# Filler products of 128 columns instead of 512 in a fused attention and feed-forward kernel

## The chip, the cores and the metric

The kernel runs on one core of one Trainium2 chip. The metric is the time of one execution on the device, in microseconds (us), as the median of several runs. The engines are TensorE (PE in the profile; its weight loads are PEld), VectorE (DVE), ScalarE (ACT), GpSimd (POOL) and SyncE (SP). Each has a queue of its own and works it off in order; they wait for each other by semaphores. TensorE writes its products into PSUM, which has eight banks; another engine must read a bank before TensorE may write it again.

## The reference

Two layers, each applied twice: memory-augmented attention in four segments, and a gated feed-forward block, both with a layer norm ahead and a residual sum behind. x is 2048 rows of 512 columns, there are 32 heads of 16 columns, and the feed-forward block is 1792 wide; everything is bfloat16. Cut to what matters:

```python
def A(x, wq, wk, wv, wo, beta):                 # x: 1 x 2048 x 512; 4 segments of 512 rows
    q, k, v = heads(x @ wq), heads(x @ wk), heads(x @ wv)
    phi = lambda t: where(t > 0, t + 1.0, exp(t))
    g = sigmoid(beta)
    for s in range(4):                          # M, z start at zero
        p = softmax(qs @ ks.T * scale + causal_mask)
        a_mem = (phi(qs) @ M) / (phi(qs) @ z + 1e-06)
        o = g * a_mem + (1.0 - g) * (p @ vs)
        M = M + phi(ks).T @ vs
        z = z + sum(phi(ks))
    return o @ wo

def B(x, w_gate, w_up, w_down):
    return (gelu(x @ w_gate) * (x @ w_up)) @ w_down

x = x + A(layernorm(x)); x = x + B(layernorm(x))
x = x + A(layernorm(x)); x = x + B(layernorm(x))
```

## The kernel before

The rows of x are worked in 8 pieces `k` = 0 to 7: four segments of 512 rows, in each of the two passes. For every piece there is an attention part (`Att`) and a feed-forward part (`Ffn`), and the parts of several pieces run interleaved, so that TensorE always has something to multiply while ScalarE works on the exponentials of the attention.

What TensorE does for a piece, in the names of the program:

- the query, key and value products (`wq_sb`, `wk_sb`, `wv_sb` with the normed and transposed rows `xnT`), by `product` (lines 471 and 476);
- the scores, `score_round` (line 938): small products of 16 or 32 rows that run side by side in strips of the array. They write four banks at a time, ScalarE takes their exponential into `pt` (line 1396), GpSimd or VectorE masks it (lines 1343, 1348, 1353);
- the flush, `flush_item` (line 954): `pt` times the values `vaug` and `vz`, in four columns of the array. VectorE turns the result (`byq`, line 971) and divides it by the sums;
- the memory's update, `upd_item`, which multiplies `phik` and the values; `phik` is turned by a DMA from SP (line 437). VectorE makes `mblk` of it and copies it to `macc` (line 893);
- the output product with `wo_sb`, the gate, up and down products with `wg_sb`, `wu_sb` and `wd_sb`; ScalarE or VectorE evicts the gate (`evict`, lines 461 and 462);
- turns of normed rows by TensorE itself for some pieces (`turn_item`, lines 584 and 586): two products of 256 columns that nobody reads, four transposes, and so on. ScalarE or VectorE then copies the result to `xnT`.

The order on every engine is written out when the kernel is built. `order` runs a model of the five engines: `ck.pe` is the planned time of TensorE, each product adds its planned cost (`Clocks.MM`, 0.2158 us for 512 columns, 0.056 for 128), and the other engines' jobs get planned times from their own costs. The main loop (from line 1423) picks what TensorE does next: scores when two rounds are ready and ScalarE has little left, else the next product of the open item, else a new item with a free bank. Changing between whole products, rows and columns of the array is planned at 0.109 us.

Where nothing is ready by the plan, a bank is free and scores are still to come (`streams` is not empty), the loop lays in a product that nobody reads: `warm` (128 x 128, all ones) times `wide`, which is `warm` read four times over, 512 columns into the free bank (line 1462). If the array stands in columns, or is about to, `product` cuts it into four products of 32 columns of the array that run side by side, each with 512 columns of data. The plan adds 0.2158 us and marks the bank as free again just after. Where no bank is free or no scores are left, the plan moves on by 0.05 us without a product.

At the start, 15 products of the same kind are made ahead of the first data (`keep_warm`, line 349); these and the ones in the turns (line 584) are not touched.

Of the kernel before, what the change touches and what calls it, by code (L numbers as in the profile page):

```python
# [18 lines left out]
P = 128  # L19
# [266 lines left out]
def order(pol, nc, cst, seg, wrk, psp, A_x, A_wq, A_wk, A_wv, A_wo, A_beta, B_x, B_w_gate, B_w_up, B_w_down, out):  # L286
# [51 lines left out]
    warm = cst.tile([P, P], BF16, name="warm")  # L338
    wide = warm[:].unsqueeze(1).to_broadcast([P, 4, P])
# [125 lines left out]
    def product(out, lhsT, rhs, start=True, stop=True):  # L465

        if ck.mode == "columns" or ck.mode == "rows" and (any(it.kind == "flush" and it.near() for it in items)):
            ck.tiling("columns")
            for c in range(4):
                r = slice(32 * c, 32 * c + 32)  # L470
                nc.tensor.matmul(out[r], lhsT=lhsT[:, r], rhs=rhs, start=start, stop=stop, tile_position=(0, 32 * c))  # L471
            ck.count += 4
        else:
            ck.tiling("whole")
            ck.count += 1
            nc.tensor.matmul(out, lhsT=lhsT, rhs=rhs, start=start, stop=stop)  # L476
# [797 lines left out]
    def next_e():  # L1274
        if not e_slots.free or e_slots.queue or phase[0] is not None:
            return
        now = streams[0][0] + streams[0][1] / STEPS if streams else 1e9
        act = ck.act
        idle = act.free <= ck.pe and act.table == "exp" and not act.only and not any(j[0] <= ck.pe and not j[4] for j in act.jobs)
        got = [j for j in e_jobs if j[1] <= ck.pe and j[2]() and (idle or j[0] <= now)]  # L1280
        if got:
            job = min(got, key=lambda j: j[0])
            e_jobs.remove(job)
            job[3](job[1], pol.e_slack)
            ck.serve()
# [17 lines left out]
    def tight():  # L1303

        return any(slot_free[slot_of(k, t)] is None for k, t in streams[2:4])
# [7 lines left out]
    def rounds_now(idle=False):  # L1313

        if not streams or phase[0] is not None and phase[1] > pol.hold or not rounds_ready(2):
            return 0
        n, left = len(free_pairs()), len(streams)
        wait = backlog()
        if n >= 2 and (idle or left <= 4 or wait < (pol.early if streams[0][0] < 1 else pol.starve)):
            return 2  # L1320
        return 0

    def pick():

        got = [i for i in range(BANKS) if banks[i] <= ck.pe]
        if not got:
            return None
        mine = sum(banks[i] > ck.pe for i in range(BANKS) if i not in score_banks)
        if streams and mine >= pol.cap and backlog() < pol.near and rounds_ready(2):
            return None  # L1330
        apart = {i for i in range(BANKS) if i not in score_banks and banks[i] > ck.pe + pol.soon} if streams else ()
        return min(got, key=lambda i: (-len(pairs_of(set(range(BANKS)) - {i, *apart})), banks[i]))

    def open_item(got, bank):
        it = min(got, key=lambda it: it.due())
        items.remove(it)
        it.ps.bank = bank
        banks[bank] = 1e9
        return it
# [83 lines left out]
    while streams or items or opened or ck.busy():  # L1423
        assert ck.pe < 2000.0, (streams[:1], [(it.kind, it.due()) for it in items[:9]], e_jobs[:2], banks)
        pol.move(ck.pe)
        ck.dve.shun = pol.shun
        ck.serve()
        next_e()
        n = rounds_now()
        if n:  # L1430
            score(n)
            continue
        if opened:
            cost, fn = opened.ops.pop(0)
            fn()
            ck.on_pe(cost)
            if not opened.ops:
                it, opened = opened, None
                it.done()
            continue  # L1440
        bank = pick()
        if bank is not None:
            late = ck.pe - pol.flush_wait
            for ck.back in (pol.lag, 0.0):
                got = [it for it in items if it.after in ev and it.ready() and (
                    it.kind != "flush" or not streams or tight() or it.posted < late or ck.mode == "columns")]
                if got:
                    break
            ck.back = 0.0
            if got:  # L1450
                opened = open_item(got, bank)
                continue

        n = rounds_now(True)
        if n:
            score(n)
            continue
        if bank is not None:
            if streams:
                ps = Psum()  # L1460
                ps.bank = bank
                product(ps(), warm[:], wide)
                ck.on_pe(Clocks.MM[512])
                ps.read(ck.pe)
                ck.fills.append(ck.pe)
                continue
        ck.pe += 0.05
        ck.stalls.append(ck.pe)
# [3 lines left out]
@with_exitstack  # L1472
def kernel(
    ctx: ExitStack,
    tc: tile.TileContext,
    A_x: bass.AP,
    A_wq: bass.AP,
    A_wk: bass.AP,
    A_wv: bass.AP,
    A_wo: bass.AP,  # L1480
    A_beta: bass.AP,
    B_x: bass.AP,
    B_w_gate: bass.AP,
    B_w_up: bass.AP,
    B_w_down: bass.AP,
    out: bass.AP,
):
    cst = ctx.enter_context(tc.tile_pool(name="cst", bufs=1))
    seg = ctx.enter_context(tc.tile_pool(name="seg", bufs=1))
    wrk = ctx.enter_context(tc.tile_pool(name="wrk", bufs=2))  # L1490
    psp = ctx.enter_context(tc.tile_pool(name="psp", bufs=1, space=bass.MemoryType.PSUM))
    ctx.enter_context(tc.manual_schedule(engines=MANUAL))
    order(Policy(POLICY, CHANGES), tc.nc, cst, seg, wrk, psp, A_x, A_wq, A_wk, A_wv, A_wo, A_beta, B_x, B_w_gate, B_w_up, B_w_down, out)
# [31 lines left out]
```

## Time and profile before

| | |
|---|---|
| time, median of 3 runs | 546.05 us (546.04 to 547.07) |
| the profiled execution's own time | 545.75 us |
| its span, first to last instruction | 544.0 us |
| mean granted clock of TensorE in it | 0.999 |
| TensorE busy | 531.3 us (98% of the span) |
| VectorE busy | 443.7 us (82%) |
| ScalarE busy | 434.7 us (80%) |
| GpSimd busy | 305.5 us (56%) |

The profile is one execution. A matmul's row shows when it started and how long it took until its last result; the next one starts before that, so the distance from start to start is what a product costs in a dense stream. A row of the timeline merges instructions of one kind that follow each other: start, time from the first start to the last end, engine and line, output and inputs, shape, count, and in brackets the idle time ahead of it with what ended it. What is named there is the last semaphore event before the start; it need not be the one that was needed. In the chain of waits the profile goes back from the last instruction, at each step to what released it or to its predecessor on the same engine. Some records of matmuls are missing (9273 products stand beside 9334 weight loads). The windows give, for a stretch, its length, the busy time and count of an engine, the mean granted clock, and the DMA engines' share and rate.

### The profile page before, as it was taken

To read this page: it belongs to the slowest core of one execution; us is meant where nothing else is said; L and a number is where in the kernel's file an instruction comes from. 1 tells how busy PE (TensorE), PEld (TensorE's weight loads), DVE (VectorE), ACT (ScalarE), POOL (GpSimd) and SP (SyncE) were. 2 spreads that over 40 slices of the span, in tenths; PEclk is the share of its full clock that TensorE was granted. 3 is DMA by queue.
4 is the path that set the end of the run, shared out by engine and by line. 5 is a ranking of instruction groups with operands and counts; after the bars stand their busy time and mean duration, and the time that the engine had idled before them with its cause. 6 is when DMAs were issued, how large, how long until landed. Compare 5 with 4: busy or idle time off the path is not lost.

```text
span 544.0 us, 21276 instructions
## 1 busy us (share of the span) xinstructions
PE 531.3 (98%) x9273; PEld 276.3 (51%) x9334; DVE 443.7 (82%) x816; ACT 434.7 (80%) x540; POOL 305.5 (56%) x359
## 2 busy tenths in 40 slices
PE   8999999999999999999999999999999999999997
PEld 4454555454545444554545555545465456555444
DVE  6998999799988999779987998889586797786342
ACT  5999989988898989989899798996879977920330
POOL 4898786369746788339993468716753265300000
PEclk9999999999999999999999999999999999999999
DMA  8406511610331123310312250221320114100001
GB/s 249 117 13 192 118 20 13 176 33 22 45 56 21 26 40 58 44 40 7 41 32 49 33 72 3 41 32 23 78 52 3 22 21 82 24 3 22 19 0 40
DMA packets 64926, 26.95 MB, mean 50 GB/s; under 512 B 49216, under 2 KB 64832, under 8 KB 64832
## 3 DMA queue, kind: packets, MB, share of 16 engines
q1 hardware_dynamic: 64400, 25.31, 22.6%
q8 instruction: 73, 1.20, 0.9%
q10 hardware_dynamic: 432, 0.27, 0.2%
q14 instruction: 21, 0.17, 0.1%
HBM read 9.71 MB, written 2.10 MB: 22 GB/s over the span
## 4 chain that ended last, share of the span: by engine, by line
PE 88%; DVE 7%; DMA 2%; issue 2%; ACT 0%; ACTq 0%; SPq 0%; DVEq 0%
PE ps L476 46%; PE ps L471 26%; PE ps L938 8%; PE ps L954 7%; DVE st L514 1%; DVE x_sb L1027 1%; DMA beta_bc<-in_A_beta_dram 1%; DVE byq L971 1%; PE ps L586 1%; DVE phiq L745 1%; PE ps L584 1%; DMA phik<-e 0%; DMA amT<-am 0%; DVE xn L544 0%; DVE e L764 0%
## 5 line engine op out<-in xcount | busy, mean ns | idle before, releaser
L1396 ACT ACTIVATE pt<-ps 128x1024 bf16<-128x1024 f32 x288 | 278.9, 1025 | 44.6 <-PE ps L938 41.1
L1343 POOL TENSOR_SCALAR_AFFINE_SELECT pt<-pt 128x256 bf16<-128x256 bf16 (+1 forms) x192 | 107.0, 571 | 118.0 <-ACT pt L1396 112.0
L1092 DVE TENSOR_TENSOR gel_sb<-gel_sb,ps 128x512 bf16<-128x512 bf16 x112 | 75.3, 682 | 33.9 <-PE ps L476 25.0
L476 PE MATMUL ps<-xnT,wu_sb 128*128 128x512 bf16 x287 | 66.8, 379 | 1.4 <-issue 1.1
L476 PE MATMUL ps<-xnT,wg_sb 128*128 128x512 bf16 x261 | 62.6, 379 | 0.9 <-issue 0.5
L764 POOL TENSOR_SCALAR e<-e 128x512 bf16<-128x512 bf16 x37 | 57.9, 1565 | 1.8 <-ACT e L741 0.7
L971 DVE STREAM_TRANSPOSE byq<-ps 128x512 f32<-128x512 f32 x64 | 45.0, 706 | 16.5 <-PE ps L954 15.9
L476 PE MATMUL ps<-wd_sb,gel_sb 128*128 128x512 bf16 (+1 forms) x293 | 56.8, 340 | 1.3 <-issue 1.0
L1348 POOL TENSOR_SCALAR_AFFINE_SELECT pt<-pt 64x1024 bf16<-64x1024 bf16 x40 | 47.8, 1196 | 15.0 <-ACT pt L1396 13.7
L1027 DVE TENSOR_TENSOR x_sb<-x_sb,ps 128x512 bf16<-128x512 bf16 (+1 forms) x68 | 42.8, 640 | 16.3 <-PE ps L476 14.7
L471 PE MATMUL ps<-wd_sb,gel_sb 128*32 128x512 bf16 (+1 forms) x792 | 47.1, 378 | 0.3 <-issue 0.3
L476 PEld LDWEIGHTS <-wu_sb 128*128 128x128 bf16 x301 | 28.2, 98 | 33.8 <-issue 0.7
L471 PE MATMUL ps<-xnT,wg_sb 128*32 128x512 bf16 x700 | 42.4, 380 | 0.0
L514 DVE BATCH_NORM_STATS2 st<-x_sb 128x6 f32<-128x512 bf16 x60 | 40.4, 674 | 0.4 <-DMA x_sb<-in_A_x_dram 0.3
L476 PEld LDWEIGHTS <-wg_sb 128*128 128x128 bf16 x273 | 25.3, 98 | 28.8 <-issue 0.2
L476 PEld LDWEIGHTS <-gel_sb 128*128 128x128 bf16 x306 | 28.3, 98 | 22.7 <-issue 1.1
L954 PE MATMUL ps<-pt,vaug 128*32 128x256 bf16 (+2 forms) x1344 | 34.6, 238 | 0.0
L417 POOL TENSOR_SCALAR kx<-kf,masks 128x512 bf16<-128x512 bf16 x20 | 33.5, 1678 | 1.2
L471 PE MATMUL ps<-xnT,wu_sb 128*32 128x512 bf16 x588 | 34.1, 379 | 0.0
L1151 ACT ACTIVATE gel_sb<-gel_sb 128x2048 bf16<-128x2048 bf16 (+1 forms) x21 | 33.2, 1643 | 0.0
L544 DVE TENSOR_SCALAR xn<-x_sb,mv,rs 128x512 bf16<-128x512 bf16 x58 | 31.3, 592 | 2.2 <-POOL rs L532 1.9
L954 PEld LDWEIGHTS <-vaug 128*32 128x32 bf16 x1344 | 27.8, 97 | 10.4 <-issue 2.2
(147 smaller groups left out, 883.6 us busy)
## 6 DMA issues: line engine op xcount, KB each, us to landing
vz<-vaug SPq DMA_DIRECT2D x14, 136.0 KB, 2.9
wg_sb<-in_B_w_gate_dram SPq DMA_DIRECT2D x8, 224.0 KB, 4.6
wu_sb<-in_B_w_up_dram SPq DMA_DIRECT2D x8, 224.0 KB, 4.3
wd_sb<-in_B_w_down_dram SPq DMA_DIRECT2D x7, 256.0 KB, 4.2
x_sb<-in_A_x_dram SPq DMA_DIRECT2D x3, 512.0 KB, 7.3
out_dram<-x_sb SPq DMA_DIRECT2D x12, 128.0 KB, 1.8
xnT<-xn SPq DMA_TRANSPOSE x40, 2.5
wk_sb<-in_A_wk_dram SPq DMA_DIRECT2D x2, 256.0 KB, 6.0
```

What stands on the lines that cost most here:

```text
L471: nc.tensor.matmul(out[r], lhsT=lhsT[:, r], rhs=rhs, start=start, stop=stop, tile_position=(0, 32 * c))
L476: nc.tensor.matmul(out, lhsT=lhsT, rhs=rhs, start=start, stop=stop)
L514: nc.vector.bn_stats(out=self.st6[:, 0, :], in_=x_sb[:, self.tt0 + j, :])
L764: lambda eng: eng.tensor_scalar(out=e[0][:], in0=e[0][:], scalar1=1.0, scalar2=None, op0=ALU.min), summed)
L938: nc.tensor.matmul(ps_all[:, bank, o + c0:o + c0 + n], lhsT=lhsT, rhs=self.q[rows, b, q0:q0 + n], start=True, stop=True, tile_position=(32 ...
L954: nc.tensor.matmul(ps()[32 * j:32 * j + 32, q0:q0 + n], lhsT=va[:, ki * VW + g:ki * VW + g + 32], rhs=pt_all[:, places[i], j, c0:c0 + n], ...
L971: nc.vector.transpose(out=self.byq[:, par, :, :].rearrange("p a c -> p (a c)"), in_=ps()[:])
L1027: ck.dve.post(ck.made(), slack, (0.15 + 0.00104 * (c1 - c0), lambda: nc.vector.tensor_tensor(out=xt, in0=xt, in1=ps()[:, 0:c1 - c0], op=AL ...
L1092: ck.dve.post(ck.made(), NORMAL, (0.683, lambda: nc.vector.tensor_tensor(out=g, in0=g, in1=ps()[:], op=ALU.mult), lambda t: (ps.read(t), e ...
L1343: nc.gpsimd.affine_select(out=view, in_=view, pattern=[[0, 4], [0, n], [1, C]], compare_op=ALU.is_ge, fill=0.0, base=C, channel_multiplier=-1)
L1348: nc.gpsimd.affine_select(out=view, in_=view, pattern=[[0, 4 * TPS], [1, C]], compare_op=ALU.is_ge, fill=0.0, base=0, channel_multiplier=-1)
L1396: nc.scalar.activation(out=pt_all[:, s0:s0 + 2, 2 * p:2 * p + 2, :].rearrange("p r h c -> p h r c"), in_=ps_all[:, pair[0]:pair[1] + 1, :] ...
```

## The change

The product that is laid in where the plan has nothing else takes 128 columns of `warm` instead of 512, and writes the first 128 columns of the bank. The planned cost stays that of 512 columns, so the plan, and with it the number, place and order of all instructions on all engines, stay as they were: 19 whole products and 48 in columns (12 groups of four) have a shorter operand, and that is the only difference between the two programs.

```diff
             if streams:
                 ps = Psum()
                 ps.bank = bank
-                product(ps(), warm[:], wide)
+                product(ps()[:, 0:P], warm[:], wide[:, 0, :])
                 ck.on_pe(Clocks.MM[512])
                 ps.read(ck.pe)
                 ck.fills.append(ck.pe)
```

## The prediction

> **What bounds the kernel now.** I read the page first, then the group of the products that read `warm`, then the chain of waits from 70 to 82 us, the timeline around every place where these products stand, and last the windows with the granted clock.
>
> ```profile
> span 544.0 us, 21276 instructions
> ...
> PE 531.3 (98%) x9273; PEld 276.3 (51%) x9334; DVE 443.7 (82%) x816; ACT 434.7 (80%) x540; POOL 305.5 (56%) x359
> ...
> PEclk9999999999999999999999999999999999999999
> ...
> PE 88%; DVE 7%; DMA 2%; issue 2%; ACT 0%; ACTq 0%; SPq 0%; DVEq 0%
> ```
>
> TensorE is busy for 98% of the span and carries 88% of the chain that ended last, at full clock. So time taken out of TensorE's stream is time gained, but only where the next product doesn't wait for somebody else. That is the whole question here: the products that are shortened (I call each a fill) stand exactly where the program's author expected nothing else to be ready.
>
> ```profile
> L471 PE MATMUL ps<-warm x48: 377/379/380, 73.8 to 135.7; 128*32 128x512 bf16 x48
> ...
> L476 PE MATMUL ps<-warm x19: 376/379/390, 21.8 to 140.1; 128*128 128x512 bf16 x19
> ```
>
> These are all of them: 19 whole fills and 48/4 = 12 that are cut into four columns of the array, 31 in all, between 21.8 and 140 us. After 140 us there is none, so the last 400 us can only inherit what is gained before.
>
> ```profile
> 69.46 2.45 DMA phik<-e
> 71.91 0.05 issue
> ...
> 73.56 1.73 PE ps L471 x50
> 75.29 0.33 PE ps L938 x12
> 75.62 1.40 PE ps L476 x6
> ...
> 79.93 0.22 PE ps L586 x4
> 80.15 0.65 PE ps L476 x3
> ```
>
> In this chain the fills lie on the path: 75.62 is six of them, 80.15 is three (0.65/3 = 0.216 us each, first start to next start). Four products of 128 columns take 0.22 us (79.93), 0.055 each. The chain says what ended last, not what would be late next.
>
> **The change part by part.** Number, places and order of all instructions stay; the planner still charges the long cost, so nothing else moves on any queue, SP's and POOL's included. One fill costs 0.216 - 0.056 = 0.160 us less, so the gross saving is 31 x 0.160 = 4.96 us. In column mode the four run side by side, so a group counts once: (1.47 - 0.38)/5 = 0.22 us per group in the row at 73.82 below. What is left is found place by place, by following each wait behind a fill to the instruction that it needs.
>
> ```profile
> 33.19 0.38 PE L586 MATMUL ps<-ident,xn 128*128 128x128 bf16 x4 [0.26 <-DVE byq L971]
> ...
> 72.98 1.94 ACT L1396 ACTIVATE pt<-ps 128x1024 bf16<-128x1024 f32 x2 [0.46 <-PE ps L938]
> ...
> 73.82 1.47 PE L471 MATMUL ps<-warm 128*32 128x512 bf16 x24
> 75.22 0.40 PE L938 MATMUL ps<-q,kf 16*128 16x64 bf16 x12
> 75.55 1.47 PE L476 MATMUL ps<-warm 128*128 128x512 bf16 x6
> ...
> 76.95 0.67 DVE L893 COPY macc<-ps 128x512 f32<-128x512 f32 x1
> ...
> 77.95 0.29 PE L938 MATMUL ps<-q,kf 16*128 16x64 bf16 x8
> ```
>
> *Two fills at 21.8.* At most 0.32 us; TensorE then sits idle at 33.19 for DVE (0.26). Taken as 0.
>
> *Three fills just before the memory update.* Behind them the update's weights wait for the transposed `phik`, which lands at 71.91 (the chain's first rows). 0.48 us becomes idle time there: 0. If that transfer came earlier, the ceiling is 0.48.
>
> *Six groups at 73.82, six whole fills at 75.55.* Gross 12 x 0.160 = 1.92. After the first six the scores need banks that the exponentials leave at 72.98 + 1.94 = 74.92; with 0.05 for the wait they begin at 74.97 instead of 75.22: 0.25 left. After the next six the flush may begin early, but the scores behind it need the bank that DVE's L893 copies out until 76.95 + 0.67 = 77.62. They begin at 77.66 instead of 77.95: 0.29 us left of 1.92. DVE runs this copy in its own order behind work that no fill feeds, so it doesn't move.
>
> ```profile
> 78.47 1.94 ACT L1396 ACTIVATE pt<-ps 128x1024 bf16<-128x1024 f32 x2 [0.28 <-PE ps L938]
> 80.30 0.60 ACT L462 ACTIVATE xnT<-ps 128x512 bf16<-128x512 bf16 x1
> ...
> 80.73 0.40 PE L938 MATMUL ps<-q,kx 32*128 32x256 bf16 x12
> 81.06 0.39 PE L476 MATMUL ps<-warm 128*128 128x512 bf16 x1
> 81.29 0.38 PE L476 MATMUL ps<-xnT,wg_sb 128*128 128x512 bf16 x1
> ...
> 86.79 1.02 ACT L1396 ACTIVATE pt<-ps 128x1024 bf16<-128x1024 f32 x1 [0.71 <-PE ps L938]
> ...
> 91.42 0.63 ACT L462 ACTIVATE gel_sb<-ps 128x512 bf16<-128x512 f32 x1
> ...
> 91.91 0.61 PE L476 MATMUL ps<-xnT,wg_sb 128*128 128x512 bf16 x2
> ```
>
> *Three fills at 79.98, one at 81.06.* Gross 0.64 on top of 0.29. ACT's exponentials at 78.47 wait for the scores, so ACT is early by the same 0.29. The gate products at 81.29 need the last `xnT`, evicted by ACT until 80.90, or 80.61 when early; so they start at about 80.66, 0.63 early. This lead over ACT isn't kept: the second product of the pair at 91.91 (it starts at 91.91 + 0.61 - 0.38 = 92.14) needs the bank that ACT's eviction leaves at 91.42 + 0.63 = 92.05; with 0.05 for the wait it has only 0.04 us to spare. TensorE can't be further ahead there than ACT. ACT is ahead by 0.29 at least; it sits idle 0.71 us for scores at 86.79 and can take more of TensorE's lead there, up to what the exponentials before left of it, some 0.44. I take 0.40, near the upper end, since 0.71 is longer than any lead.
>
> *One fill ahead of the second update.* The fill itself waits for a bank, and the products behind it for `phik` again: 0 of 0.16.
>
> ```profile
> 133.76 1.94 ACT L1396 ACTIVATE pt<-ps 128x1024 bf16<-128x1024 f32 x2 [0.21 <-PE ps L938]
> ...
> 134.59 1.47 PE L471 MATMUL ps<-warm 128*32 128x512 bf16 x24
> ...
> 136.00 0.40 PE L938 MATMUL ps<-q,kf 16*128 16x64 bf16 x12
> ...
> 136.83 0.23 PEld L586 LDWEIGHTS <-xn 128*128 128x128 bf16 x4 [0.40 <-DVE xn L544]
> ...
> 138.49 1.57 ACT L462 ACTIVATE xnT<-ps 128x512 bf16<-128x512 bf16 x3
> ...
> 139.83 0.60 PE L476 MATMUL ps<-warm 128*128 128x512 bf16 x2
> 140.27 0.38 PE L476 MATMUL ps<-xnT,wg_sb 128*128 128x512 bf16 x1
> ```
>
> *Six groups at 134.59.* Gross 0.96. The scores may come 0.25 us earlier (exponentials end at 133.76 + 1.94 = 135.70), but the turns at 136.83 wait for DVE's `xn`, already with idle time: 0 beyond the 0.40 that DVE carries itself.
>
> *One fill before the scores, two at 139.83.* Gross 0.48. The gate products need ACT's third `xnT`, at 138.49 + 1.57 = 140.06; with 0.05 they start at 140.11 instead of 140.27: 0.15.
>
> Sum: 0.40 + 0.15 = 0.55 us; 4.4 of the gross 4.96 turn into idle time. The profiled execution took 545.75 us (544.0 of span and 1.75 around it), 0.3 below the median of 546.05; against the median the sum gives 545.5.
>
> **The rivals.** About 0.2%, 1.1 us, is what a measurement of this kernel can tell from no change.
>
> *The clock drops (slower).* Emptier stretches may halve TensorE's clock.
>
> ```profile
> 3.94:7.35 3.41, 2.67 (x17) 1.00 0.78 212
> ...
> 73.82:77.23 3.41, 3.41 (x70) 1.00 0.02 5
> ...
> 539.83:543.24 3.41, 1.04 (x10) 1.00 0.14 39
> 543.00:544.00 1.00, 0.00 (x0) 0.62 0.00 0
> ```
>
> In these windows (length, busy time, products, then the clock) the clock stays full with 2.67 of 3.41 us busy, and falls to half after the end: 0.62 over the last microsecond is 0.24 us at full and 0.76 at half speed, so it fell at 543.24, 2.4 us after the last product, at the end of 3.41 us with 1.04 busy. The changed kernel's emptiest such stretch lies between 74 and 78 us: pauses of some 0.6 us before the scores at 74.97, up to 0.8 us around the flush and before the scores at 77.66, and the gaps between; about 1.7 of 3.41 us are left busy. That lies between the kept and the lost case. One half-speed stretch of 3.41 us costs 1.7 us of products: 545.5 + 1.7 = 547.2. It decides once the clock falls in most executions. Against it: every pause is short, 0.6 us beside the 2.4 us at the end. Chance 0.18.
>
> [...]
>
> *The waits move along (faster).* If DVE and ACT come earlier too, the lead of 0.63 at 81.29 is kept, the scores' 0.25 after 134.59 is added, and 0.15 at the end: 1.03, and a little from the zeros above; 545.0 to 544.7. Read literally, the chain gives all 4.96: 541.1. For it speaks that the chain shows hardly anything but PE from 71.95 to 82; against it, each pin above is an end of ACT, DVE or a transfer. Chance 0.11, little of it for 541.1.
>
> *Nothing is left (within 0.2%).* A later wait for ACT or DVE eats the 0.55, since ACT is busy for 80% and DVE for 82% of the span: 546.0. Chance 0.20.
>
> **How the numbers follow.** Forecast 0.51, nothing left 0.20, clock 0.18, waits moving 0.11. The predicted time is that of the forecast, 545.5. The first two lie within 0.2%: 0.71 the same; 0.11 faster; 0.18 slower. The range 544.8 to 547.2 takes in the zeros' ceilings below (0.48 and 0.25 more than the forecast) and reaches to one lost stretch of clock.
>
> **What would show it.** In the changed profile the fills' groups have 128 columns and some 0.22 us each; idle time appears on PE before the update at 71.9 (DMA), before the scores near 74.9 (ACT) and 77.6 (DVE), at 136.4 (DVE) and 140.1 (ACT). TensorE's busy time falls by about 4 us while the span falls by about half of one. The gate products that stood at 81.29 stand near 80.7, those of 91.91 near 91.5, those of 140.27 near 139.7. If the clock rival holds, the clock shows 0.5 in a stretch between 75 and 85 us, and everything behind stands later than before. The prediction is wrong if DVE's copy L893 moves, if the clock falls, or if the lead at 140 us isn't found at the end.

## The result, and the profile after

The changed kernel takes 545.10 us (median of 15 runs, 544.58 to 545.95); the kernel before, run beside it on the same chip, 546.04 us (15 runs, 545.50 to 547.07). The ratio is 0.9984, with a 95% interval of 0.9977 to 0.9991: the change saves 0.94 us, and between 0.5 and 1.25 by that interval. 545.5 was forecast, 0.55 us below the 546.05 of before. The time is within 0.2% of before, as forecast, and the gain is somewhat larger than the sum. Run a second time, on another chip, the changed kernel was 0.9990 of before (0.9981 to 0.9999). Of a gross saving of 4.96 us, about a fifth arrives.

The page of the changed kernel, whose profiled execution took 545.07 us:

```profile
span 543.4 us, 21276 instructions
...
PE 528.7 (97%) x9273; PEld 276.3 (51%) x9334; DVE 443.8 (82%) x816; ACT 434.4 (80%) x540; POOL 306.2 (56%) x359
...
PEclk9999999999999999999999999999999999999999
...
PE 83%; DVE 10%; ACT 3%; issue 2%; DMA 2%; ACTq 0%; DVEq 0%
```

The number of instructions is the same, TensorE's clock is still full (1.000 in the mean), and TensorE's busy time has fallen from 531.3 to 528.7 us while the span has fallen by 0.6. In the chain TensorE's share falls from 88 to 83%, VectorE's rises from 7 to 10 and ScalarE's from 0 to 3: the time that the fills gave back is now waited for elsewhere. The fills themselves, by the program's name `warm`:

```profile
L471 PE MATMUL ps<-warm x48: 216/219/230, 73.8 to 134.4; 128*32 128x128 bf16 x48
...
L476 PE MATMUL ps<-warm x19: 216/219/230, 21.6 to 139.1; 128*128 128x128 bf16 x19
```

(minimum, median and maximum in ns, then the first and last start). From start to last result a fill takes 219 ns instead of 379. Where TensorE now waits, from the waits by engine (us in total, times, longest):

```profile
PE ps L476 <- DMA phik<-e: 1.2, 2, 0.8
...
PE ps L938 <- ACT pt L1396: 0.7, 2, 0.4
...
PE ps L586 <- DVE xn L544: 0.4, 1, 0.4
PE ps L938 <- DVE macc L893: 0.3, 1, 0.3
...
PE ps L476 <- ACT xnT L462: 0.2, 1, 0.2
```

These are the five waits that the prediction named: the transposed `phik`, ScalarE's exponentials, VectorE's `xn` and its copy L893, ScalarE's `xnT`. The timeline of TensorE shows where they stand:

```profile
71.97 0.59 PE L476 MATMUL ps<-gel_sb,phik 128*128 128x128 bf16 x7 [0.78 <-DMA phik<-e]
...
73.83 0.64 PE L471 MATMUL ps<-warm 128*32 128x128 bf16 x24
74.40 0.20 PE L938 MATMUL ps<-q,kf 16*128 16x64 bf16 x2
74.98 0.40 PE L938 MATMUL ps<-q,kf 16*128 16x64 bf16 x10 [0.37 <-ACT pt L1396]
75.31 0.51 PE L476 MATMUL ps<-warm 128*128 128x128 bf16 x6
...
77.32 0.27 PE L938 MATMUL ps<-q,kf 16*128 16x64 bf16 x5 [0.28 <-DVE macc L893]
...
80.30 1.89 PE L476 MATMUL ps<-xnT,wg_sb 128*128 128x512 bf16 x7
```

The scores that stood at 75.22 run from 74.98 (74.97 was forecast); those of 77.95 wait for L893. And the chain of waits, which ran along TensorE from 71.95 to 82 before, now runs along VectorE there:

```profile
75.59 0.56 DVE zcols L882
76.16 0.52 DVE xn L544
76.68 0.59 DVE macc L893
77.27 1.27 DVE xn L544 x3
```

To see where the gain comes from and where it goes, each instruction of TensorE in the one trace is set beside the same instruction in the other. The table gives start in the kernel named, less start in the kernel before (us; less than zero is earlier), at times of the kernel before. It is worked out from the starts in the traces, one execution each; it isn't a view of the profile.

```
  at    changed   changed   first 5   12 at     4+1 at    last 9    stands
                  (again)             73.8      80/112.7            ahead of
  20.0   -0.19     -0.34     -0.09     -0.42     -0.17     +0.18    the first fill
  22.5   -0.36     -0.51     -0.26     -0.42     -0.17     +0.18    two fills
  69.0   -0.36     -0.51     -0.26     -0.42     -0.17     +0.18
  72.0   +0.01     -0.38     -0.17     -0.21     +0.14     +0.02    phik's transfer
  75.4   -0.25     -0.64     -0.17     -0.48     +0.15     +0.02    exponentials
  78.0   -0.65     -0.81     -0.17     -0.72     +0.15     +0.02    copy L893
  81.3   -0.99     -1.15     -0.17     -0.73     -0.19     +0.01    ACT's xnT
  83.4   -0.80     -0.96     -0.17     -0.73      0.00     +0.01    ACT's exponentials
 112.0   -0.80     -0.96     -0.17     -0.73      0.00     +0.02
 113.3   -0.50     -0.90     +0.32     -0.74     +0.35     -0.06    phik's 2nd transfer
 134.0   -0.62     -1.01      0.00     -0.75     +0.22     -0.09
 136.2   -0.87     -1.26      0.00     -0.75     +0.22     -0.34    exponentials
 137.1   -0.62     -1.01     -0.29     -0.75     +0.22     -0.08    DVE's xn
 143.0   -0.77     -1.17     -0.29     -0.75     +0.22     -0.24    ACT's xnT
 540.0   -0.65     -1.12     -0.30     -0.75     +0.37     +0.17    the end
```

Two things are read from it beside the steps. Already at 20 us, ahead of the first fill, executions differ by up to 0.6 us: that is the start-up, not the change. And where a transfer sets TensorE's start (72.0 and 113.3), the shift changes by up to 0.5 us, differently in each execution and mostly by a loss of lead, since the transfers didn't land at the same time (the row at 72.0 has them from 0.38 us earlier to 0.14 later than before). One trace can therefore be read to 0.1 us between two such places, not from end to end.

### The profile page after: what moved, and what is told of

It reads as the page before. It is cut to its first block, busy times and chain, and to the rows that moved or that the text cites. A ratio compares the mean times of both kernels' runs of the same rounds, so it can differ in the third digit from the quotient of the medians.

```text
span 543.4 us, 21276 instructions
## 1 busy us (share of the span) xinstructions
PE 528.7 (97%) x9273; PEld 276.3 (51%) x9334; DVE 443.8 (82%) x816; ACT 434.4 (80%) x540; POOL 306.2 (56%) x359
## 4 chain that ended last, share of the span: by engine, by line
PE 83%; DVE 10%; ACT 3%; issue 2%; DMA 2%; ACTq 0%; DVEq 0%
PE ps L476 43%; PE ps L471 26%; PE ps L938 7%; PE ps L954 6%; DVE st L514 2%; ACT pt L1396 2%; DVE x_sb L1027 1%; DMA beta_bc<-in_A_beta_dram 1%; DVE byq L971 1%; DVE xn L544 1%; DMA phik<-e 1%; DVE phiq L745 1%; DVE mv L522 0%; DVE e L745 0%; ACT xnT L462 0%
```

## The experiments

**The fills of one place at a time.** Four kernels make the fills short in one group of places and leave all others long: the first 5 (two at 21.8, three before the update), the next 12 (73.8 to 76.9), the next 5 (four at 80, one at 112.7) and the last 9.

```diff
-                product(ps(), warm[:], wide)
+                if len(ck.fills) < 5:          # or 5 to 16, 17 to 21, from 22
+                    product(ps()[:, 0:P], warm[:], wide[:, 0, :])
+                else:
+                    product(ps(), warm[:], wide)
```

> Only the first five fills are shortened (two at 21.8 us, three at 71.0 us). The prediction's reckoning: both places give 0, because TensorE waits for VectorE at 33.2 us and for the transfer of phik at 71.9 us; time as before, within 0.1 us, and beyond 82 us no lead that was not there at 20 us. Rival, from the changed kernel's trace: the wait at 33.2 us moves along, since VectorE's work there is itself fed by TensorE; then TensorE and VectorE are some 0.16 us earlier from 34 to 70 us, TensorE loses it at 71.9 us, VectorE keeps it, and it comes back to TensorE at 77.9 us, where TensorE waits for VectorE: 0.15 us faster at the end. Clock: 1.0 throughout by both.

> Only the twelve fills of 73.8 to 76.9 us are shortened, 1.92 us gross. The prediction's reckoning: VectorE's copy L893 doesn't move, the scores behind it come 0.29 us earlier, and this lead is found at 81 us and at the end: about 0.3 us faster. Rival, all waits move along: over 1 us earlier at 78 us and faster by over 1 us. Rival, the emptier stretch costs clock: a stretch at half clock between 75 and 85 us and 1.5 us slower.

> Only the four fills of 80.0 to 81.1 us and the single one at 112.7 us are shortened, 0.80 us gross. The prediction's reckoning with ACT not moved: the scores at 80.73 come 0.27 us earlier (they wait for the exponentials that end at 80.41), the gate products at 81.29 some 0.34 earlier, and at 92.1 us, where TensorE stands 0.04 us behind ACT's eviction, what is left is 0.04 to 0.15, if ACT takes up the lead at its pause of 0.7 us at 86.8. At the end 0.04 to 0.15 us faster, too little for the times. Rival, all waits move along: 0.64 us lead from 81.3 us to the end.

> Only the last nine fills (six groups at 134.6 us, one at 139.2, two at 139.8) are shortened, 1.44 us gross. The prediction's reckoning: the six give 0.25 us at the scores at 136.0 and nothing at 136.8, where TensorE waits for VectorE's xn; the last three give 0.15 us at the gate products at 140.27, which wait for ACT's xnT; 0.15 us lead from there to the end, 0.15 us faster. Rival, the waits move along: 0.7 us or more.

Medians, with the kernel before at 545.99 on the same chip: first five 545.59, ratio 0.9995 (0.9986 to 1.0004); next twelve 545.45, 0.9992 (0.9984 to 1.0001); next five 545.99, 1.0000 (0.9991 to 1.0009); last nine 545.87, 0.9995 (0.9987 to 1.0004). No part alone is told from no change by its time. The four differences add up to -0.18%, where the whole measured -0.16%, so nothing large arises only when they are together. What each part does has to be read from its trace, and there the steps are sharp.

*First five.* In all three traces of this table in which the two fills at 21.8 are short, TensorE gains 0.17 us at that place (-0.19 to -0.36, -0.34 to -0.51, -0.09 to -0.26); in the three in which they are long the shift stays put. The prediction had this gain lost at 33.19, where TensorE sits idle for VectorE. The kernel before and the changed one, in the timeline of TensorE:

```profile
21.75 0.59 PE L476 MATMUL ps<-warm 128*128 128x512 bf16 x2
22.18 0.81 PE L476 MATMUL ps<-wv_sb,xnT 128*128 128x512 bf16 x2
```

```profile
21.56 0.28 PE L476 MATMUL ps<-warm 128*128 128x128 bf16 x2
21.82 0.82 PE L476 MATMUL ps<-wv_sb,xnT 128*128 128x512 bf16 x2
...
32.84 0.38 PE L586 MATMUL ps<-ident,xn 128*128 128x128 bf16 x4 [0.26 <-DVE byq L971]
```

The product behind the two fills comes 0.26 instead of 0.43 us after the first of them: 0.17 of the gross 0.32 is left. And the wait at 33.19 is still 0.26 long, at 32.84: VectorE's `byq` came 0.35 earlier too, since it reads what TensorE makes. The idle time was there before and is there after; the gain went past it. In the kernel with only the first five short it doesn't come back at 77.9 us, as the rival had expected: the transfer leaves TensorE at -0.17, VectorE's copy L893 is at -0.20 and not awaited. The two fills help TensorE behind the transfer only where VectorE is what it waits for next.

*Next twelve.* TensorE's rows of that kernel:

```profile
74.75 0.40 PE L938 MATMUL ps<-q,kf 16*128 16x64 bf16 x10 [0.37 <-ACT pt L1396]
75.08 0.51 PE L476 MATMUL ps<-warm 128*128 128x128 bf16 x6
...
77.25 0.27 PE L938 MATMUL ps<-q,kf 16*128 16x64 bf16 x5 [0.28 <-DVE macc L893]
```

At the scores 0.27 us are gained (-0.21 to -0.48; 0.25 was forecast). At 78.0 TensorE is at -0.72 where VectorE, by the starts of its copy L893, is at -0.43 from the start-up on: 0.29 more than VectorE, which is the forecast's figure. So the copy is the pin, as written.

*Next five.* From 72.0 to the gate products at 81.3 the shift goes from +0.14 to -0.19, 0.33 gained (0.34 was forecast: 0.63 less 0.29). Two us on, 0.14 of it is left. The prediction put the end of the lead over ScalarE near 92, with "the exponentials before" as an upper bound of 0.44; the trace has the lead cut at 83.44 already, by such exponentials: there the gate's first group in columns needs a bank that ScalarE's exponentials leave. The kernel before and the changed one, the timelines of ScalarE and TensorE:

```profile
81.29 1.95 ACT L1396 ACTIVATE pt<-ps 128x1024 bf16<-128x1024 f32 x2
...
83.44 1.05 PE L471 MATMUL ps<-xnT,wg_sb 128*32 128x512 bf16 x16
```

```profile
80.64 1.95 ACT L1396 ACTIVATE pt<-ps 128x1024 bf16<-128x1024 f32 x2
...
82.64 1.05 PE L471 MATMUL ps<-xnT,wg_sb 128*32 128x512 bf16 x16
```

Before, the exponentials end at 83.24 and the group starts at 83.44; with 0.05 for the wait it had 0.15 to spare. In the changed kernel they end at 82.59 and the group starts at 82.64, at the pin. In the kernel with only these five fills short ScalarE isn't earlier than at 72.0, and just this spare time is left (0.14 by the shifts). At the second update, at 113, the transfer takes that too.

*Last nine.* Three rows of TensorE:

```profile
135.66 0.40 PE L938 MATMUL ps<-q,kf 16*128 16x64 bf16 x10 [0.37 <-ACT pt L1396]
...
136.75 0.40 PE L586 MATMUL ps<-ident,xn 128*128 128x128 bf16 x4 [0.37 <-DVE xn L544]
...
140.03 1.24 PE L476 MATMUL ps<-xnT,wg_sb 128*128 128x512 bf16 x5 [0.17 <-ACT xnT L462]
```

0.25 is gained at the scores, all of it is lost at VectorE's `xn`, and 0.16 is gained at ScalarE's `xnT` (-0.08 to -0.24): 0.25, 0 and 0.15 were forecast.

**Each fill made twice.** If the fills stood beside slack, twice the work would cost little.

```diff
                 product(ps(), warm[:], wide)
+                product(ps(), warm[:], wide)
```

> Every fill of 512 columns is made twice: 31 x 0.216 = 6.7 us more on TensorE. Theory of the waits: the fills fill gaps that end within some tenths of a us, so doubling them is paid nearly in full: of 6.7 us only the idle times that stand behind fills before (0.27 us at 71.9, 0.40 at 136.8 and the slack of a few tenths at 33.2) hide some; 5 to 6.5 us slower, 551 to 552.5. Rival, the fills stand in slack of their own: under 2 us slower.

551.54 us against 546.19: ratio 1.0103 (1.0089 to 1.0118), 5.35 us. The added fills are 31 x 0.216 = 6.7 us gross. A row of it, where six stood in the kernel before:

```profile
78.26 2.76 PE L476 MATMUL ps<-warm 128*128 128x512 bf16 x12
```

By the shift of starts 6.5 us had been added at 390 us and 5.9 at the end (of the 0.65 between these two, below). So a longer fill costs nearly its whole length, and a shorter one gives back a fifth. Before, TensorE meets the others' ends with 0 to 0.35 us to spare, and behind that the pins wait.

**The pin at L893 taken away.** The changed kernel, with VectorE's copy to `macc` ahead of `zcols` in the update, so that the bank is free some 1.1 us earlier (before, `zcols` starts at 75.87 and the copy at 76.95):

```diff
-                             (Port(0.2), z, told),
-                             (0.683, lambda: nc.vector.tensor_copy(out=macc[:], in_=blocks()), psm.read)]
+                             (Port(0.2), lambda: nc.vector.tensor_copy(out=macc[:], in_=blocks()), told),
+                             (0.683, z, psm.read)]
```

> The changed kernel, with VectorE's copy into macc ahead of the small product zcols instead of behind it (two instructions of the memory's first update change places in VectorE's queue, in two pieces). VectorE's copy then ends some 0.6 us earlier, and the wait of 0.28 us at 77.3 us goes. If that wait alone bounds the lead there, the scores and with them all that follows come 0.28 us earlier. If ACT is next late (its queue has no idle time left before the exponential at 77.8 us), the scores come 0.28 us earlier but the exponential, the scores at 79.6 and the gate products at 80.3 do not: under 0.1 us at 82 us and at the end.

544.77 us against 546.19: 0.9980 (0.9971 to 0.9989), not told from the changed kernel's 0.9984 (0.9977 to 0.9991). TensorE's rows, and then the chain of waits of the same kernel:

```profile
76.67 0.30 PE L954 MATMUL ps<-pt,vaug 128*32 128x64 bf16 x8 [0.24 <-POOL pt L1343]
...
77.34 0.29 PE L938 MATMUL ps<-q,kf 16*128 16x64 bf16 x8
```

```profile
77.99 1.74 ACT pt L1396 x2
...
79.80 0.56 ACT xnT L462
...
80.80 1.98 ACT pt L1396 x2
...
82.81 0.38 PE ps L471
```

The wait for the copy is gone: the eight scores run without a pause. In this trace the gain is nothing all the same. Counted from 72.0, where the transfer sets TensorE's start, TensorE is 1.00 us earlier at 81.3 (+0.18 to -0.82), and so it is in the changed kernel (+0.01 to -0.99); at 83.4 it is 0.81 in both. With VectorE's copy out of the way ScalarE is late at the same moment: from 77.99 on the chain goes along it, up to the exponentials that the group in columns waits for (80.80 + 1.98 = 82.78, and 82.81). So in the changed kernel's first trace two pins stood at the same place. Each trace is one execution: in the second one ScalarE still sat idle for 0.12 us ahead of that exponential, and there the copy alone was the pin.

**No fills at all.** The choice of how the array is cut is kept, the products are left out, the plan is unchanged. What is left out is read by nobody. The same kernel was profiled three times: once in its timed runs, and twice more on another chip.

```diff
-                product(ps(), warm[:], wide)
+                if (ck.mode == "columns" or ck.mode == "rows"
+                        and any(it.kind == "flush" and it.near() for it in items)):
+                    ck.tiling("columns")
+                else:
+                    ck.tiling("whole")
```

> The 31 fills are left out altogether; the plan still charges 0.2158 us for each, so all else keeps its order. They feed nothing, so no part of the result is missing. Theory of the waits: places that wait for ACT, VectorE or a transfer behind the fills start as in the changed kernel; only where nothing is waited for does the last 0.056 us of a fill go too (0.1 us at 21.8 us). So within 0.2 us of the changed kernel, 0.6 to 1.0 us faster than before, clock 1.0 throughout. Clock rival: the stretches at 74 to 77 us and 134 to 137 us are emptier than in the changed kernel, a window at half clock appears there in the trace, and the time is 1 to 3 us longer than the changed kernel's.

> The kernel without fills once more, for its trace alone. In the first look the clock stood at half from 78.05 to 81.47 us, after a stretch of 3.41 us (74.64 to 78.05) with 2.24 us busy. If the clock is set by stretches of 3.41 us that lie on a grid of their own, it falls in this execution only where a stretch of the grid has about 2.2 us busy or less, which the start of the grid decides (stretches that begin at 73.0 to 74.6 us have 1.8 to 2.1 us busy, one that begins at 75.1 to 76 has 2.5 to 2.8): half clock for 3.41 us behind it, about 1.05 us lost, or none at all. Rival, the clock falls after a pause of a certain length: then in every execution at the same place.

> A third look at the kernel without fills, with the same expectations as for the second: by the grid, half clock for 3.41 us where a stretch of the grid has about 2.2 us busy or less, full clock throughout where none has; by the pause, half clock in every execution from the same place.

545.25 us against 546.19: 0.9984 (0.9974 to 0.9994), as much as with short fills; the second and the third profiled execution took 546.14 and 544.49. The windows of the first, by the steps of the clock (length, busy time of TensorE, products, clock, DMA), and rows of its timeline:

```profile
74.64:78.05 3.41, 2.24 (x80) 1.00 0.02 5
78.05:81.47 3.42, 3.35 (x34) 0.50 0.00 0
81.47:84.88 3.41, 3.22 (x44) 1.00 0.00 0
```

```profile
74.93 0.40 PE L938 MATMUL ps<-q,kf 16*128 16x64 bf16 x10 [0.71 <-ACT pt L1396]
...
76.38 0.29 PE L954 MATMUL ps<-pt,vaug 128*32 128x64 bf16 x8 [0.61 <-POOL pt L1343]
...
77.53 0.27 PE L938 MATMUL ps<-q,kf 16*128 16x64 bf16 x5 [0.27 <-DVE macc L893]
...
78.52 0.64 PE L586 MATMUL ps<-ident,xn 128*128 128x128 bf16 x4
```

Here is the clock rival. For one stretch of 3.41 us, behind one in which TensorE was busy for 2.24 us, the clock is half; four transposes that take 0.39 us take 0.64. The second profile shows the same at 78.12 to 81.54, behind a stretch with 1.78 busy. The third kept its clock; its stretches are counted from the steps of the clock at its start and end:

```profile
71.52:74.93 3.41, 2.25 (x89) 1.00 0.00 0
74.93:78.35 3.42, 2.40 (x82) 1.00 0.02 5
```

The third has the same pauses at the same places (0.71, 0.66 and 0.27 us, where the first has 0.71, 0.61 and 0.27), so a rule by the length of a pause alone falls. By the shift of starts, a half-speed stretch costs 1.06 us in the first (-0.45 at 78.0, +0.61 at 79.9) and 1.39 in the second profile; in the third there is no step. Some of it comes back: at 83.4 the first is at +0.45 and the second at +1.28, 1.05 and 1.25 us lost beside the third, which gains 0.15 from 78.0 to there. The mean granted clock of each run tells the same without a trace: 0.997 is 0.003 x 544 = 1.6 us of clock missing, half of one such stretch (0.999 is the end of the span alone: in the kernel before, 0.76 us at half speed behind 543.24). The run of 546.35 has 0.993, enough for two such stretches.

```
no fills          clock full      544.23 544.41 544.49 544.55
                  0.997 or less   545.15 545.21 545.25 545.33 545.62 545.62 546.14 546.19 546.35
twelve short      clock full      544.09 to 545.02 (9 runs), 543.94 to 544.87 (5 runs)
                  0.997           545.47 545.91, 545.86
all 31 short      clock full      25 runs (two measurements of the changed kernel)
                  0.997           547.34
```

So the clock fell in 9 of 13 runs without fills, in 3 of 17 with the twelve alone, and in 1 of 26 with all of them short. Without fills and with a full clock the kernel takes some 544.4 us, with a fall some 1 us more, and the median lands by chance where the short fills stand.

**Only the twelve short fills, none elsewhere.** The twelve at 73.8 to 76.9 short, as in the experiment on them, and the other 19 left out in the way of the last one. Beside its second run, the changed kernel again.

```diff
-                product(ps(), warm[:], wide)
+                if 5 <= len(ck.fills) < 17:
+                    product(ps()[:, 0:P], warm[:], wide[:, 0, :])
+                elif ...                       # as with no fills at all
```

> Only the twelve fills of 73.8 to 76.9 us are made, with 128 columns; the other 19 are left out (they feed nothing, so the result is whole). The waits: where the 19 stood TensorE waits for others or gains at most 0.056 us per place, so the time is within 0.2 us of the changed kernel. The clock: from 73 to 79 us the stretches are as full as in the changed kernel (2.8 us or more of 3.41 busy), so it stays at 1.0 there; a fall could come only for a stretch that begins near 133.7 us (2.3 us busy without fills).

> The kernel with only the twelve fills of 73.8 to 76.9 us, short. The waits: within 0.2 us of the changed kernel beside it, so that the 1.5 us of its first measurement against before was in part chance. Rival, the 19 fills left out cost something of their own: 0.5 us or more faster than the changed kernel.

> The changed kernel again, on the same chip as the one with twelve short fills alone, to compare the two and to see how far its traces differ. The waits: as in its first measurement 0.5 to 0.95 us faster than before; in the trace, 0.29 us lead of TensorE over VectorE at 78 us, some 0.44 at 92 us, 0.15 more behind 140 us, and at 71.9 and 113.2 us whatever the transfer of phik makes of it.

544.52 us against 546.35, 0.9972 (0.9963 to 0.9981), and again 544.73 against 546.16, 0.9974 (0.9963 to 0.9986). The changed kernel beside the second: 545.29, 0.9990 (0.9981 to 0.9999). These are the lowest medians of the study, though the gap to the changed kernel, 0.56 us on the same chip, is not outside the intervals. Within 0.2 us was expected, so the theory of the waits missed here, and the gap has the size that the rival named, a cost of the 19 fills. Its cause by the traces is told at the end, and it isn't the fills' own time. Where the clock fell in 3 of the 17 runs is not known, since both profiled executions kept it.

## Why the prediction was right, and where its steps failed

*TensorE only gains up to the next pin: right.* 0.25 at the first scores (measured 0.27), 0.29 over VectorE at the copy L893 (0.29 with the twelve alone, 0.30 in both traces of the changed kernel, where VectorE is at -0.35 and -0.51), 0.63 less 0.29 at the gate products (0.34), nothing kept over `xn` at 137 (all of 0.25 lost), 0.15 at the last `xnT` (0.15 and 0.16).

*"This lead over ACT isn't kept": right, but at another place.* The step named the eviction that ends at 92.05, with 0.04 us to spare, bounded what passes by 0.29 and 0.44 and took 0.40. The trace shows that its upper bound, "what the exponentials before left of it", is the pin: they end at 83.24, with 0.15 to spare, and 0.30 + 0.15 = 0.45 gets past them (-0.65 at 78.0, -0.80 at 83.4), and nothing more is lost at 92, since ScalarE, idle for scores at 86.79, takes over the rest. The size came out at the upper end, because the eviction at 92 takes nothing more.

*"Two fills at 21.8 ... Taken as 0": wrong.* They give 0.17 us at their place, in three traces of three. The step took an idle time in front of an instruction for slack that swallows a gain. But the engine waited for was fed by TensorE a few us before, so it moved along. That is the mechanism of the rival "the waits move along", at the one place where no price was put on it.

*"DVE runs this copy in its own order behind work that no fill feeds, so it doesn't move": right for the fills behind 71 us, wrong for the change as a whole.* The changed kernel's row, in the timeline of VectorE, stands at 76.60 instead of 76.95:

```profile
76.60 0.67 DVE L893 COPY macc<-ps 128x512 f32<-128x512 f32 x1
```

Of these 0.35, 0.17 are the two fills at 21.8, which VectorE carries through the transfer at 72 that resets TensorE; the other 0.19 (by rounding) were there at 20 us already. The prediction had named "if DVE's copy L893 moves" as what would make it wrong; it moved, and the copy then held TensorE at its new time, so that this sign came true and the forecast held all the same: 0.17 us is small beside the range.

*Three fills before the update, and one at 112.7, taken as 0: right,* with `phik`'s transfer as the pin (0.78 us of wait at 71.97). What was not asked is whether a lead passes the second transfer. It did with the twelve alone (nothing lost), nearly so in the second trace of the changed kernel (0.06 lost), and not in the first (0.30 lost).

*The sum.* 0.40 + 0.15 = 0.55 was forecast. With 0.17 added and 0.45 in place of 0.40 it is 0.17 + 0.45 + 0.15 = 0.77, less what the second transfer takes. Both intervals (0.5 to 1.25, and 0.05 to 1.04 us) hold this; they also hold 0.55. The traces show the 0.17, the times can't. That the changed kernel's trace has 0.77 at 143 us too is chance: there the start-up's 0.19 is added and the second transfer's 0.30 lost.

*The clock rival: it exists, but didn't decide, and its price was too high.* "About 1.7 of 3.41 us are left busy" is too empty by the profile's busy time: the changed kernel's two stretches there are

```profile
70.58:73.99 3.41, 2.63 (x101) 1.00 0.20 38
73.99:77.40 3.41, 2.76 (x96) 1.00 0.02 5
```

and with 2.63 the clock holds. The prediction took the pauses as 0.6 us ahead of the first scores and up to 0.8 around the flush and the second; the profile shows 0.37 and 0.28, since a short fill counts as busy for its 0.22 us, four times the 0.055 that were taken for it, and since the flush hardly waits. One of 26 runs has the clock at 0.997, at 547.34 us; where in it the clock fell no trace shows. That it lies close to the 547.2 of that rival is luck: a half-speed stretch was put at 1.7 us and measures 1.06 and 1.39, presumably since part of it falls on time in which TensorE would have waited.

*TensorE's busy time* was said to fall by about 4 us; it fell by 2.6. The likely reason: the tails of the short products (0.22 us from start to last result, 0.055 from start to start) stick out into the new pauses, where a dense stream covers them.

*Nothing is left:* the lead at 143 us (0.77) is there at 540 (0.65, and 1.12 of 1.17 in the second trace). ScalarE and VectorE, busy for 80 and 82%, didn't eat it. That rival falls.

## What to carry to other kernels

Before an idle time is taken as slack that swallows a gain, follow the awaited engine back to what feeds it: if the engine that gains does, the wait moves along and the gain passes. Where an order is planned to meet several engines' ends closely, shortening a filler pays only up to the next of these ends, and lengthening it costs nearly its whole length (here 0.94 of 4.96 us came back, and 5.35 of 6.7 were paid), so twice the work is no measure of what half of it will bring. Here fills of 128 columns, 0.22 us each from start to last result, were enough for a full clock in 25 of 26 runs, though TensorE still paused there for up to 0.37 us; without any fill the clock fell in 9 of 13 runs, and a median over few runs can't tell that from a gain that isn't there: read the granted clock of every run. How short such a filler may be is not known beyond the 128 columns tried here.

## What the runs showed of the hardware

**The clock fell with no pause over 0.71 us.** In the first profile of the kernel without fills the longest pause within the stretch ahead of the fall is 0.61 us (the 0.71 at 74.93 lies in part before the stretch), with 2.24 of 3.41 us busy; in the second it is 0.71, with 1.78 busy. Stretches of the same kind of small products with 2.25 and 2.40 busy kept the clock, in the third. The steps of the clock stand 3.41 us apart in the first and the second (78.05 and 81.47, 78.12 and 81.54). In the kernel before, the clock's record has it full from 3.94 to 543.24 us, which is 539.31 us or 158 times 3.413; in the changed kernel it is full from 5.72, for the same 539.31. So the steps seen in these traces fit a grid of 3.413 us, whose offset differs from one execution to the next: counted from the start of the span it is 0.52 us in the kernel before, 2.31 in the changed one, and 2.96, 3.03 and 3.25 in the three without fills, of which the first two lost the clock and the third kept it. This fits that the same program fell in some runs and not in others.

The busy time that the profile shows doesn't tell the lost stretches from the kept ones, though. The first profile of the kernel without fills ends with products of 256 columns in a dense row, the last of them 1.49 us before the end of a stretch. That stretch and the rest of the span:

```profile
538.85:542.27 3.42, 1.92 (x18) 1.00 0.22 71
542.27:543.90 1.63, 0.00 (x0) 1.00 0.04 12
```

With 1.92 busy the clock held, where the same execution had lost it with 2.24; in the changed kernel's first profile the last such stretch (538.20 to 541.62) held with 2.02. The difference may be the tails: a product of 128 columns is busy for some 0.219 us and costs 0.055 from start to start, so some 0.164 us of it is tail, and the lost stretch has 80 small products in its 2.24 us, the kept one 18 in 1.92. That is an estimate from these numbers; no run was made to test it, and none shows at which busy time the clock falls.

**A pause at 398 us that goes with the number of instructions.** The kernel before, in the middle of products of one kind, 258 us behind the last fill:

```profile
398.07 1.48 PE L471 MATMUL ps<-wd_sb,gel_sb 128*32 128x512 bf16 x24 [0.31 <-issue]
```

and the kernel with only twelve fills:

```profile
396.90 2.62 PE L471 MATMUL ps<-wd_sb,gel_sb 128*32 128x512 bf16 x44
```

"issue" means that nothing in the profile was waited for. All eight traces of kernels with the number of instructions of before have this pause, 0.21 to 0.73 us of TensorE's idle time, behind the same product; the six traces of kernels with fewer or more (no fills, twelve fills, fills twice) don't, and against before their starts step forward there by 0.65 to 0.67 us (-0.36 to -1.03 and -0.27 to -0.94 with twelve fills; +6.54 to +5.87 with fills made twice). So most of what the twelve-fill kernel has over the changed kernel, 0.56 us on the same chip, and the 0.65 that the doubled fills give back, is this pause. Why is open. Loads of instructions by DMA stand 1.6 to 2.1 us before it (at 395.67 and 396.13), but the kernel with twelve fills has such loads at the same place (395.86 and 396.23) and no pause.
